# Windowed attention with sink tokens, then a rational feed-forward: attention rebuilt over head pairs with DMA transposes

## The chip, the cores and the metric

The kernel runs on one core of a Trainium2 chip. The metric is device time in microseconds (us) of one execution. The core has five engines: PE (matmul, with PEld for its weight loads), DVE (vector), ACT (scalar), POOL (GpSimd) and SP, which only issues transfers here; transfers run on the core's 16 DMA engines.

## What is computed

Four batches of eight heads, 768 positions, head dimension 64. Each position attends to the 128 positions up to itself and to the first four positions (the sinks). The attended values are laid out as 3072 tokens of 512 numbers and go through a feed-forward of width 2048, whose activation is a ratio of polynomials.

```python
scores = scale * np.matmul(q, k.transpose(0, 1, 3, 2))
keep = is_sink | in_window            # column < 4, or 0 <= row - column < 128
scores = np.where(keep, scores, -1e9)
a = softmax(scores)                   # over the last axis
x = np.matmul(a, v)                   # then heads are laid side by side: 3072 x 512
h = x @ w_in                          # 512 x 2048
P = a0 + a1*h + a2*h**2 + a3*h**3
Q = 1 + abs(b0)*abs(h) + abs(b1)*h**2
out = (P / (Q + 1e-6)) @ w_out        # 2048 x 512
```

## The kernel before

*Prologue (lines 44 to 125).* POOL builds the identity and masks, then issues the 16 transfers of `w_out` (L82), then those of the coefficients `moe_a` and `moe_b` (L86, L88). DVE computes small constants from them (L90 to L110) and casts the four pieces of `w_in` (L118), whose staging tiles `t_f` live in a pool of two buffers that is closed afterwards. The result of attention is collected in four tiles `xT`, each with the 128 columns of two heads on its partitions.

*Attention (lines 129 to 227).* One loop over batches and heads. Q, K and V of a head are loaded as 128 positions by 6 tiles (L142 and L144 on SP, L143 on ACT), cast to bf16 (L148 ACT, L149 DVE, L151 POOL), and Q and K are transposed on PE against the identity (L159, L160), six blocks each, and copied out of PSUM (L161, L162). Per head there is one matmul of the four sink keys against 512 queries (L165, exponential L168), and 11 score matmuls of 128 keys by 128 queries (L188), in three groups of two query tiles: each group has one exponential of up to 512 columns (L191) and one mask multiplication, on DVE for the first group (L195), on POOL for the two others (L198). For each query tile up to three matmuls gather the values (L203 own tile, L206 the tile before, L210 sinks), with a column of ones that gives the sum of the weights; the reciprocal (L214) scales the result (L217 on ACT or L220 on DVE), PE transposes it (L223), and once per head DVE copies it into `xT` (L226).

*Feed-forward (lines 229 to 327).* 24 units of 512 tokens by 512 hidden columns. PE multiplies by `w_in` (L258), ACT copies out (L262, tile `hb`), DVE forms numerator and denominator (L272 to L284), ACT the reciprocal by logarithm and exponential (L289, L292), DVE the product `g_t` (L321); PE multiplies by `w_out` (L300), ACT copies (L303) and SP stores (L305).

*What sets the order.* The framework places the instructions and their waits: on each engine they stand in an order that follows the program text and the readiness of operands, and an engine executes its own list in order. A tile of a pool takes over the buffer of an older tile of the same tag and waits for that tile's last reader; a pool opened after another was closed may take over its memory and waits for it.

## Time and profile before

| | us |
|---|---|
| median of 3 runs (486.37 to 487.19) | 486.61 |
| the profiled execution, whole time | 487.0 |
| its span, first to last instruction | 485.3 |
| PE busy | 392.3 |
| DVE busy | 300.5 |
| ACT busy | 295.7 |
| POOL busy | 102.3 |

Busy times are sums over instructions of one engine; a matmul's end is modelled, and matmuls overlap, so PE's time is not a measure of work at full rate. The slices divide the span in 40 equal parts, each digit a busy share in tenths. In a table by stretches, an engine's column gives busy time and the number of instructions; the last columns are the granted PE clock (1.00 is 2.4 GHz), the busy share of the DMA engines (above 1 where an engine's packets overlap) and the traffic in GB/s. In a timeline or a group an arrow names what ended the idle time ahead of the instruction.

### The profile page before, as it was taken

The numbers are of one execution on the slowest core, as the hardware profiler recorded it, in microseconds if no ns is written. First come the engines' busy times: TensorE is split into PE (matmuls) and PEld (weight loads), VectorE is DVE, ScalarE is ACT, GpSimd is POOL, SyncE is SP. The second block draws the span as 40 slices with busy tenths as digits, with TensorE's granted clock in tenths as the row PEclk, the third lists the DMA queues.
The fourth block names the chain that finished last, engine by engine and source line by source line (L and its number), as shares of the span: only waits on it lengthen the run. The fifth ranks groups of instructions, "written<-read, shape, count | busy, mean of one in ns | idle before, by whom it ended". The sixth has DMA issues, their size and how long they took to land.

```text
span 485.3 us, 6228 instructions
## 1 busy us (share of the span) xinstructions
PE 392.3 (81%) x2208; PEld 205.1 (42%) x2208; DVE 300.5 (62%) x627; ACT 295.7 (61%) x416; POOL 102.3 (21%) x155
## 2 busy tenths in 40 slices
PE   0018989887887888888897897789999999999866
PEld 0015545554554555545554533234444344443322
DVE  0223443445444445445435429999999999999970
ACT  1005645644555554555564527989979898898951
POOL 6202442424333342442434310000000000000000
PEclk9999999999999999999999999998999999999979
DMA  9778232342332242324223000001010010110102
GB/s 249 153 210 134 67 69 63 82 113 50 83 82 66 67 97 66 83 50 97 67 65 82 2 0 1 0 1 66 22 43 26 19 66 22 43 45 4 62 22 86
DMA packets 81695, 31.86 MB, mean 66 GB/s; under 512 B 76032, under 2 KB 78080, under 8 KB 81152
## 3 DMA queue, kind: packets, MB, share of 16 engines
q1 hardware_dynamic: 54208, 23.07, 17.7%
q10 hardware_dynamic: 25088, 6.29, 6.0%
q0 software_dynamic: 2368, 2.10, 2.7%
q8 instruction: 17, 0.28, 0.2%
q14 instruction: 14, 0.11, 0.1%
HBM read 27.27 MB, written 6.29 MB: 69 GB/s over the span
## 4 chain that ended last, share of the span: by engine, by line
PE 44%; DVE 40%; DMA 6%; issue 5%; ACT 3%; POOL 1%; DVEq 0%; ACTq 0%; POOLq 0%
PE ps_s L188 8%; PE ps_xall L223 7%; DVE g_t L321 5%; DVE odd L283 5%; DVE num L284 5%; PE ps_tk L160 5%; PE ps_o L203 5%; PE ps_tq L159 5%; PE ps_o L210 4%; PE ps_out L300 4%; DVE s_sq L272 4%; DVE num L281 4%; PE ps_sink L165 3%; DVE odd L278 3%; DVE den L273 3%
## 5 line engine op out<-in xcount | busy, mean ns | idle before, releaser
L300 PE MATMUL ps_out<-w_out_sb,g_t 128*128 128x512 bf16 x384 | 94.5, 395 | 16.0 <-DVE g_t L321 13.7
L258 PE MATMUL ps_h<-xT,w_in_sb 128*128 128x512 bf16 x384 | 93.8, 392 | 3.0 <-ACT hb L262 3.0
L214 DVE RECIPROCAL recip<-ps_o 128x1 f32<-128x1 f32 x192 | 29.6, 164 | 92.0 <-PE ps_o L210 84.6
L198 POOL TENSOR_TENSOR a_t<-e_t,mask_pp 128x512 bf16<-128x512 bf16 x64 | 73.9, 1161 | 59.1 <-ACT e_t L191 58.6
L160 PE MATMUL ps_tk<-ident,k_bf 128*64 128x128 bf16 x192 | 37.5, 313 | 47.3 <-DVE k_bf L149 45.6
L217 ACT ACTIVATE o_bf<-ps_o,recip 128x64 bf16<-128x64 f32 x96 | 30.0, 313 | 64.3 <-DVE recip L214 63.6
L300 PEld LDWEIGHTS <-g_t 128*128 128x128 bf16 x384 | 37.8, 101 | 68.3 <-DVE g_t L321 22.8
L191 ACT ACTIVATE e_t<-ps_s 128x512 bf16<-128x512 f32 (+1 forms) x96 | 52.4, 556 | 19.5 <-PE ps_s L188 17.0
L289 ACT ACTIVATE lnq<-den,one_eps,qsc 128x2048 f32<-128x2048 bf16 x24 | 50.3, 2096 | 19.8 <-DVE den L276 19.7
L223 PE MATMUL ps_xall<-ident,o_bf 128*64 128x128 bf16 x192 | 52.5, 314 | 9.7 <-ACT o_bf L217 5.7
L258 PEld LDWEIGHTS <-w_in_sb 128*128 128x128 bf16 x384 | 38.0, 100 | 51.2 <-issue 9.8
L262 ACT ACTIVATE hb<-ps_h 128x1024 bf16<-128x1024 f32 x48 | 48.6, 1012 | 6.0 <-PE ps_xall L223 3.3
L188 PE MATMUL ps_s<-qT,kT 64*128 64x128 bf16 x352 | 50.5, 304 | 0.2 <-ACT e_t L191 0.2
L203 PE MATMUL ps_o<-v_ext,a_t 128*128 128x65 bf16 x192 | 40.3, 237 | 8.8 <-DVE a_t L195 8.5
L160 PEld LDWEIGHTS <-k_bf 128*64 128x64 bf16 x192 | 23.5, 160 | 52.6 <-DVE k_bf L149 48.7
L292 ACT ACTIVATE rden<-lnq 128x2048 bf16<-128x2048 f32 x24 | 45.7, 1903 | 0.0
L223 PEld LDWEIGHTS <-o_bf 128*64 128x64 bf16 x192 | 24.8, 143 | 37.4 <-ACT o_bf L217 13.9
L206 PE MATMUL ps_o<-v_ext,a_t 128*128 128x65 bf16 x160 | 39.2, 245 | 0.0
L151 POOL CAST v_ext<-v_in 128x384 bf16<-128x384 f32 x32 | 16.2, 506 | 100.2 <-PE ps_o L210 67.7
L188 PEld LDWEIGHTS <-kT 64*128 64x128 bf16 x352 | 31.3, 130 | 11.8 <-issue 8.2
L159 PE MATMUL ps_tq<-ident,q_bf 128*64 128x128 bf16 x192 | 33.9, 314 | 0.0
L161 ACT ACTIVATE qT<-ps_tq 64x768 bf16<-64x768 bf16 x32 | 25.5, 797 | 13.3 <-PE ps_tq L159 10.6
(61 smaller groups left out, 495.3 us busy)
## 6 DMA issues: line engine op xcount, KB each, us to landing
q_in<-in_q_dram SPq DMA_DIRECT2D x32, 192.0 KB, 3.1
k_in<-in_k_dram ACTq DMA_DIRECT2D x32, 192.0 KB, 2.8
v_in<-in_v_dram SPq DMA_DIRECT2D x32, 192.0 KB, 2.8
out_dram<-o_t SPq DMA_DIRECT2D x24, 256.0 KB, 2.0
t_f<-in_moe_w_in_dram SPq DMA_DIRECT2D x4, 1024.0 KB, 5.7
w_out_sb<-in_moe_w_out_dram POOLq DMA_DIRECT2D x16, 128.0 KB, 5.9
a_bc<-in_moe_a_dram POOLq DMA_DIRECT2D x1, 2.0 KB, 4.5
b_bc<-in_moe_b_dram POOLq DMA_DIRECT2D x1, 1.0 KB, 4.0
```

What stands on the lines that cost most here:

```text
L159: nc.tensor.transpose(ps_tq[:, t * P:(t + 1) * P], q_bf[:, t, :], ident)
L160: nc.tensor.transpose(ps_tk[:, t * P:(t + 1) * P], k_bf[:, t, :], ident)
L188: nc.tensor.matmul(ps_s[:, co:co + P], lhsT=kT[:, kt * P:(kt + 1) * P], rhs=qT[:, t * P:(t + 1) * P], start=True, stop=True)
L191: nc.scalar.activation(out=e_t[:, 0:ncols], in_=ps_s[:, 0:ncols], func=AF.Exp)
L198: nc.gpsimd.tensor_tensor(out=a_t[:, 0:ncols], in0=e_t[:, 0:ncols], in1=pmask, op=ALU.mult)
L203: nc.tensor.matmul(ps_o, lhsT=a_t[:, col[(t, 'diag')]:col[(t, 'diag')] + P], rhs=v_ext[:, t, :], start=True, stop=(t == 0))
L223: nc.tensor.transpose(ps_xall[:, t * P:(t + 1) * P], o_bf, ident)
L258: nc.tensor.matmul(ps_h[:, j, :], lhsT=w_in_sb[c][:, fc * P:(fc + 1) * P], rhs=xT[c][:, t0:t0 + TB], start=(c == 0), stop=(c == NDMC - 1))
L262: nc.scalar.activation(out=hb[:, half * 2 * TB:(half + 1) * 2 * TB], in_=ps_h, func=AF.Copy)
L289: nc.scalar.activation(out=lnq, in_=den, func=AF.Ln, scale=qsc, bias=one_eps)
L292: nc.scalar.activation(out=rden, in_=lnq, func=AF.Exp, scale=-1.0)
L300: nc.tensor.matmul(ps_out, lhsT=g_t[:, co:co + P], rhs=w_out_sb[fc], start=(fc == 0), stop=(fc == NFFC - 1))
```

## The change

Constants, loads and the attention loop are replaced; the feed-forward keeps its text. Two heads are worked on together. K and V of a pair are held in 64-position halves: 64 partitions for one head, 64 for the other, in tiles that are zero outside the two diagonal blocks, so that one matmul over 128 rows serves both heads. A half of 64 keys is scored against the 192 queries that can see it; one exponential covers four halves (768 columns), with the scale 1/8 folded in, and one DVE multiplication masks the two 64-column edges of each half. Q, the block-diagonal K and the normalised output are transposed by DMA from SBUF to SBUF (`dma_start_transpose` on SP) instead of by PE with copies out of PSUM. The sink keys of all eight heads of a batch are gathered into one tile, and one set of matmuls gives all their scores. All loads are issued on SP. A loop of 21 steps runs the pairs in a pipeline: pair p+2 is loaded, p prepared, p-4 scored, p-5 attended and emitted. The cut diff (constants for the sinks and their V tile are left out; of removed lines the first of each block stand):

```diff
@@ -46,35 +46,37 @@
     wpool = ctx.enter_context(tc.tile_pool(name="weights", bufs=1))
     xpool = ctx.enter_context(tc.tile_pool(name="xT", bufs=1))
 
-    ident = const_pool.tile([P, P], BF16)
-    make_identity(nc, ident)
...
+
+    edge = const_pool.tile([P, 2, 64], BF16)
+    nc.gpsimd.memset(edge, 1.0)
+    for e in range(2):
+        lo = e * 64
+        nc.gpsimd.affine_select(
+            out=edge[lo:lo + 64, 0, :], in_=edge[lo:lo + 64, 0, :], pattern=[[1, 64]],
+            compare_op=ALU.is_ge, fill=0.0, base=0, channel_multiplier=-1)
+        nc.gpsimd.affine_select(
+            out=edge[lo:lo + 64, 1, :], in_=edge[lo:lo + 64, 1, :], pattern=[[-1, 64]],
+            compare_op=ALU.is_gt, fill=0.0, base=0, channel_multiplier=1)
+
...
+    with tc.tile_pool(name="a_fix", bufs=1) as a_fix, \
+         tc.tile_pool(name="a_in", bufs=3) as a_in, \
+         tc.tile_pool(name="a_q", bufs=2) as a_q, \
+         tc.tile_pool(name="a_qT", bufs=6) as a_qT, \
+         tc.tile_pool(name="a_x", bufs=3) as a_x, \
          tc.tile_pool(name="a_ps", bufs=2, space=bass.MemoryType.PSUM) as a_ps, \
-         tc.tile_pool(name="a_ps_tr", bufs=1, space=bass.MemoryType.PSUM) as a_ps_tr, \
          tc.tile_pool(name="a_ps_sink", bufs=1, space=bass.MemoryType.PSUM) as a_ps_sink, \
-         tc.tile_pool(name="a_ps_x", bufs=1, space=bass.MemoryType.PSUM) as a_ps_x, \
          tc.tile_pool(name="a_ps_o", bufs=2, space=bass.MemoryType.PSUM) as a_ps_o:
+
+        k_nat2 = []
+        for n in range(2):
+            t_ = a_fix.tile([P, NHF, P], BF16, name=f"k_bd_{n}")
+            nc.gpsimd.memset(t_, 0.0)
+            k_nat2.append(t_)
+        v_bd = []
+        for n in range(NVB):
+            t_ = a_fix.tile([P, NHF, 2, D + 1], BF16, name=f"v_bd_{n}")
+            nc.gpsimd.memset(t_, 0.0)
+            for e in range(2):
+                nc.gpsimd.memset(t_[e * 64:(e + 1) * 64, :, e, D:D + 1], 1.0)
+            v_bd.append(t_)
+        e_bd = []
+        for n in range(NEB):
+            t_ = a_fix.tile([P, 64 + NHF * EW], BF16, name=f"e_bd_{n}")
+            nc.gpsimd.memset(t_, 0.0)
+            e_bd.append(t_)
+        k_sink = []
+        for n in range(2):
+            t_ = a_fix.tile([P, NPB, P], BF16, name=f"k_sink_{n}")
+            nc.gpsimd.memset(t_, 0.0)
+            k_sink.append(t_)
...
+        def load(p):
+            b, i = p // NPB, p % NPB
+            q_in = a_in.tile([P, NT, 2, D], FP32, tag="q_in")
+            k_in = a_in.tile([P, NHF, D], FP32, tag="k_in")
+            v_in = a_in.tile([P, NHF, D], FP32, tag="v_in")
+            for e in range(2):
+                h = 2 * i + e
+                nc.sync.dma_start(out=k_in[e * 64:(e + 1) * 64],
+                                  in_=k[b, h].rearrange("(j p) d -> p j d", p=64))
+                nc.sync.dma_start(out=q_in[:, :, e, :],
+                                  in_=q[b, h].rearrange("(t p) d -> p t d", p=P))
+            for e in range(2):
+                h = 2 * i + e
+                nc.sync.dma_start(out=v_in[e * 64:(e + 1) * 64],
+                                  in_=v[b, h].rearrange("(j p) d -> p j d", p=64))
+            loaded[p] = (q_in, k_in, v_in)
+
+        def prepare(p):
+            b, i = p // NPB, p % NPB
+            q_in, k_in, v_in = loaded.pop(p)
+            q_bf = a_q.tile([P, NT, P], BF16, tag="q_bf")
+            nc.vector.tensor_copy(out=q_bf, in_=q_in.rearrange("p t e d -> p t (e d)"))
+            k_n = k_nat2[p % 2]
+            for e in range(2):
+                nc.scalar.activation(out=k_n[e * 64:(e + 1) * 64, :, e * D:(e + 1) * D],
+                                     in_=k_in[e * 64:(e + 1) * 64], func=AF.Copy)
+            qT = a_qT.tile([P, NT + 1, P], BF16, tag="qT")
+            kT = a_qT.tile([P, NHF, P], BF16, tag="kT")
+            nc.gpsimd.memset(qT[:, NT, :], 0.0)
+            nc.sync.dma_start_transpose(out=qT[:, 0:NT, :],
+                                        in_=q_bf.rearrange("p t c -> p (t c)"))
+            nc.sync.dma_start_transpose(out=kT, in_=k_n.rearrange("p j c -> p (j c)"))
+            nc.gpsimd.tensor_copy(
+                out=k_sink[b % 2][:, i, 32 * i:32 * i + 32].rearrange(
+                    "p (e s) -> p e s", e=2)[:, :, 0:NS],
+                in_=kT[:, 0, :].rearrange("p (e s) -> p e s", e=2)[:, :, 0:NS])
+            ready[p] = (qT.rearrange("p t c -> p (t c)"), kT, v_in)
+
+        def prepare_v(p):
+            v_in = ready[p][2]
+            v_n = v_bd[p % NVB]
+            for e in range(2):
+                nc.vector.tensor_copy(out=v_n[e * 64:(e + 1) * 64, :, e, 0:D],
+                                      in_=v_in[e * 64:(e + 1) * 64])
+
+        def sink_scores(b):
+            ps = a_ps_sink.tile([P, S - P], FP32, tag="ps_sink")
+            for c0, c1 in ((0, 512), (512, S - P)):
+                for i in range(NPB):
+                    nc.tensor.matmul(ps[:, c0:c1], lhsT=k_sink[b % 2][:, i, :],
+                                     rhs=ready[b * NPB + i][0][:, P + c0:P + c1],
+                                     start=(i == 0), stop=(i == NPB - 1))
+            e_s = a_x.tile([P, S - P], BF16, tag="e_sink")
+            nc.scalar.activation(out=e_s, in_=ps, func=AF.Exp, scale=inv_sqrt_d)
+            nc.vector.tensor_tensor(out=e_s[:, 0:NS], in0=e_s[:, 0:NS], in1=sink_edge,
+                                    op=ALU.mult)
+            sinks[b] = e_s
+
+        def scores(p, g):
+            qT, kT, _ = ready[p]
+            e_t = e_bd[p % NEB]
+            ps = a_ps.tile([P, 2, 512], FP32, tag="ps_s")
+            for n in range(4):
+                j = 4 * g + n
+                nc.tensor.matmul(ps[:, n // 2, (n % 2) * 192:(n % 2) * 192 + 192],
+                                 lhsT=kT[:, j, :], rhs=qT[:, 64 * j:64 * j + 192],
                                  start=True, stop=True)
-                e_sink = a_sc.tile([NS, (NT - 2) * P], BF16, tag="e_sink")
-                nc.scalar.activation(out=e_sink, in_=ps_sink, func=AF.Exp)
...
+            data = e_t[:, 64:].rearrange("p (j c) -> p j c", c=EW)
+            nc.scalar.activation(
+                out=data[:, 4 * g:4 * g + 4, 0:192].rearrange("p (a n) c -> p a n c", a=2),
+                in_=ps[:, :, 0:384].rearrange("p a (n c) -> p a n c", n=2),
+                func=AF.Exp, scale=inv_sqrt_d)
+            tri_blocks = data[:, 4 * g:4 * g + 4, :].rearrange(
+                "p j (m c) -> p j m c", c=P)[:, :, :, 0:64]
+            nc.vector.tensor_tensor(
+                out=tri_blocks, in0=tri_blocks,
+                in1=edge0 if g == 0 else edge.unsqueeze(1).to_broadcast([P, 4, 2, 64]),
+                op=ALU.mult)
+
+        def attend(p, g, x_n):
+            b, i = p // NPB, p % NPB
+            e_t = e_bd[p % NEB]
+            v_n = v_bd[p % NVB]
+            ps_o = a_ps_o.tile([P, 2, 2 * (D + 1)], FP32, tag="ps_o")
+            for n in range(2):
+                t = 2 * g + n
+                terms = []
+                for j, off in ((2 * t, 0), (2 * t - 1, 64), (2 * t + 1, -64), (2 * t - 2, 128)):
+                    if j >= 0:
+                        c = 64 + EW * j + off
+                        terms.append((e_t[:, c:c + P], v_n[:, j, :, :]))
+                if t > 0:
+                    terms.append((sinks[b][:, (t - 1) * P:t * P],
+                                  v_sink[:, b, 2 * i:2 * i + 2, :]))
+                for m, (l_, r_) in enumerate(terms):
+                    nc.tensor.matmul(ps_o[:, n, :], lhsT=l_,
+                                     rhs=r_.rearrange("p e c -> p (e c)"),
+                                     start=(m == 0), stop=(m == len(terms) - 1))
+            o4 = ps_o.rearrange("p n (e c) -> p (n e) c", e=2)
+            rec = a_x.tile([P, 4, 1], FP32, tag="rec")
+            nc.vector.reciprocal(out=rec, in_=o4[:, :, D:D + 1])
+            nc.vector.tensor_tensor(
+                out=x_n[:, 2 * g:2 * g + 2, :].rearrange("p n (e c) -> p (n e) c", e=2),
+                in0=o4[:, :, 0:D], in1=rec.to_broadcast([P, 4, D]), op=ALU.mult)
+
+        def emit_x(p, x_n):
+            b, i = p // NPB, p % NPB
+            nc.sync.dma_start_transpose(
+                out=xT[i][:, b * S:(b + 1) * S].rearrange("p (t c) -> p t c", c=P),
+                in_=x_n.rearrange("p t c -> p (t c)"))
+
+        for p in range(2):
+            load(p)
+        for p in range(NPAIR + 5):
+            if p + 2 < NPAIR:
+                load(p + 2)
+            if p < NPAIR:
+                prepare(p)
+            s_ = p - 4
+            if 0 <= s_ < NPAIR:
+                prepare_v(s_)
+                if s_ % NPB == 0:
+                    sink_scores(s_ // NPB)
+            a_ = p - 5
+            x_n = None
+            if 0 <= a_ < NPAIR:
+                x_n = a_x.tile([P, NT, P], BF16, tag="x_n", name="x_n")
+            for g in range(3):
+                if 0 <= s_ < NPAIR:
+                    scores(s_, g)
+                if x_n is not None:
+                    attend(a_, g, x_n)
+            if x_n is not None:
+                emit_x(a_, x_n)
 
     TB = 512
     NB = NTOK // TB

```

## Rows read from the trace of the kernel before

**Rows 1.** The page: busy per engine, and PE, DVE, DMA in 40 slices
```profile
PE 392.3 (81%) x2208; PEld 205.1 (42%) x2208; DVE 300.5 (62%) x627; ACT 295.7 (61%) x416; POOL 102.3 (21%) x155
...
PE   0018989887887888888897897789999999999866
...
DVE  0223443445444445445435429999999999999970
```

**Rows 2.** Busy time by stretch: us; PE, PEld, DVE, ACT, POOL; clock, DMA share, GB/s
```profile
0.00:30.30 30.30, 0.00 (x0) 0.00 (x0) 7.36 (x25) 1.49 (x2) 11.00 (x27) 1.00 0.79 208
30.30:288.00 257.70, 217.89 (x1451) 130.50 (x1452) 113.99 (x417) 133.69 (x289) 91.35 (x128) 1.00 0.34 74
288.00:470.00 182.00, 163.15 (x715) 69.99 (x713) 179.05 (x187) 158.11 (x122) 0.00 (x0) 0.97 0.08 29
470.00:485.30 15.30, 11.24 (x43) 4.58 (x43) 0.10 (x1) 2.39 (x4) 0.00 (x0) 0.83 0.18 69
```

**Rows 3.** Timelines at the stage edges: start us, us, engine, line, [idle before]
```profile
29.02 1.29 DVE L118 TENSOR_SCALAR w_in_sb<-t_f,csc 128x2048 bf16<-128x2048 f32 x1 [1.87 <-DMA t_f<-in_moe_w_in_dram]
30.33 0.38 SPq L142 DMA_DIRECT2D q_in<-in_q_dram  x1
...
287.95 1.02 ACT L262 ACTIVATE hb<-ps_h 128x1024 bf16<-128x1024 f32 x1 [3.32 <-PE ps_xall L223]
```

**Rows 4.** PE's timeline: two rounds of values, six transposes, eight wide matmuls
```profile
102.35 0.23 PE L203 MATMUL ps_o<-v_ext,a_t 128*128 128x65 bf16 x1
...
102.74 0.24 PE L203 MATMUL ps_o<-v_ext,a_t 128*128 128x65 bf16 x1
...
103.12 0.85 PE L159 MATMUL ps_tq<-ident,q_bf 128*64 128x128 bf16 x6
...
300.68 1.89 PE L258 MATMUL ps_h<-xT,w_in_sb 128*128 128x512 bf16 x8 [0.83 <-ACT hb L262]
```

**Rows 5.** Groups by shape: count, busy us, mean ns, idle us before with its releaser
```profile
L198 POOL TENSOR_TENSOR a_t<-e_t,mask_pp 128x512 bf16<-128x512 bf16 x64 | 73.9, 1161 | 59.1 <-ACT e_t L191 58.6
L191 ACT ACTIVATE e_t<-ps_s 128x512 bf16<-128x512 f32 x64 | 37.8, 594 | 16.4 <-PE ps_s L188 14.3 <-POOL v_ext L152 1.6 <-POOL v_ext L151 0.5
L220 DVE TENSOR_SCALAR o_bf<-ps_o,recip 128x64 bf16<-128x64 f32 x96 | 26.9, 280 | 2.4
L226 DVE COPY xT<-ps_xall 64x768 bf16<-64x768 bf16 x32 | 17.6, 549 | 15.8 <-PE ps_xall L223 15.0
L148 ACT ACTIVATE q_bf<-q_in 128x384 bf16<-128x384 f32 x32 | 16.4, 514 | 14.8 <-DMA q_in<-in_q_dram 14.8
L191 ACT ACTIVATE e_t<-ps_s 128x384 bf16<-128x384 f32 x32 | 15.4, 480 | 3.1 <-PE ps_s L188 2.6
```

**Rows 6.** Single lines on DVE: ns min/median/max, first and last start
```profile
L149 DVE CAST k_bf<-k_in x32: 340/360/897, 34.5 to 266.1; 128x384 bf16<-128x384 f32 x32
L195 DVE TENSOR_TENSOR a_t<-e_t,mask_p x32: 337/351/1142, 42.0 to 278.3; 128x384 bf16<-128x384 bf16 x32
```

**Rows 7.** The fastest stretch, and the densest of 256-byte loads (columns of rows 2)
```profile
4.00:6.00 2.00, 0.00 (x0) 0.00 (x0) 0.00 (x0) 0.00 (x0) 2.00 (x5) 1.00 1.01 426
35.00:42.00 7.00, 5.47 (x42) 4.23 (x42) 1.98 (x6) 2.52 (x5) 1.07 (x3) 1.00 1.35 218
```

**Rows 8.** DMA issues: count, KB each, us from issue to landing
```profile
q_in<-in_q_dram SPq DMA_DIRECT2D x32, 192.0 KB, 3.1
```

**Rows 9.** POOL's memsets: a 128-column constant, and 6 columns per head
```profile
masks.py:197 POOL MEMSET ident<- 128x128 bf16 x1 | 0.2, 204 | 0.3 <-POOLq L344 0.3
L152 POOL MEMSET v_ext<- 128x6 bf16 x32 | 4.0, 124 | 14.9 <-DVE w_in_sb L118 14.9
```

**Rows 10.** Waits of SP: line, releaser, us in total, times, longest
```profile
SPq L144 <- POOL v_ext L152: 105.7, 24, 7.5
```

**Rows 11.** PE's clock after a gap: timeline rows, then the stretch (columns of rows 2)
```profile
467.67 2.32 PE L300 MATMUL ps_out<-w_out_sb,g_t 128*128 128x512 bf16 x5 [4.04 <-DVE g_t L321]
...
470.00:474.00 4.00, 3.84 (x10) 1.45 (x11) 0.10 (x1) 0.60 (x1) 0.00 (x0) 0.52 0.12 44
```

More of the change, by code (lines that the diff above doesn't have):

```diff
@@ L63 @@
-    nc.gpsimd.affine_select(
-        out=mask_prev, in_=ones_pp, pattern=[[-1, P]], compare_op=ALU.is_gt,
-        fill=0.0, base=0, channel_multiplier=1,
-    )
-    mask_p0 = const_pool.tile([P, 3 * P], BF16)
-    nc.vector.tensor_copy(out=mask_p0[:, 0:P], in_=mask_diag)
-    nc.vector.tensor_copy(out=mask_p0[:, P:2 * P], in_=mask_diag)
-    nc.vector.tensor_copy(out=mask_p0[:, 2 * P:3 * P], in_=mask_prev)
-    nc.vector.memset(mask_p0[0:NS, 0:P], 1.0)
-    nc.vector.memset(mask_p0[0:NS, 2 * P:3 * P], 1.0)
@@ L73 @@
-    mask_pp = const_pool.tile([P, 4 * P], BF16)
-    nc.vector.tensor_copy(out=mask_pp[:, 0:P], in_=mask_diag)
-    nc.vector.tensor_copy(out=mask_pp[:, P:2 * P], in_=mask_prev)
-    nc.vector.tensor_copy(out=mask_pp[:, 2 * P:3 * P], in_=mask_diag)
-    nc.vector.tensor_copy(out=mask_pp[:, 3 * P:4 * P], in_=mask_prev)
+    edge = const_pool.tile([P, 2, 64], BF16)
[8 more added lines that the diff above has]
+            compare_op=ALU.is_gt, fill=0.0, base=0, channel_multiplier=1)
@@ new lines @@
+    edge0 = const_pool.tile([P, 4, 2, 64], BF16)
+    nc.gpsimd.tensor_copy(out=edge0, in_=edge.unsqueeze(1).to_broadcast([P, 4, 2, 64]))
+    for e in range(2):
+        nc.gpsimd.memset(edge0[e * 64:e * 64 + NS, 0, 0, :], 1.0)
+    tri = const_pool.tile([P, H, NS], FP32)
+    nc.gpsimd.memset(tri, 1.0)
+    nc.gpsimd.affine_select(out=tri, in_=tri, pattern=[[-16, H], [0, NS]],
+                            compare_op=ALU.is_ge, fill=0.0, base=0, channel_multiplier=1)
+    ind = const_pool.tile([P, H], FP32)
@@ new lines @@
+    nc.gpsimd.affine_select(out=ind, in_=tri[:, :, 0], pattern=[[16, H]],
+                            compare_op=ALU.is_ge, fill=0.0, base=NS - 1,
+                            channel_multiplier=-1)
+    nc.gpsimd.affine_select(out=tri, in_=tri, pattern=[[16, H], [1, NS]],
+                            compare_op=ALU.is_ge, fill=0.0, base=0, channel_multiplier=-1)
+    sink_edge = const_pool.tile([P, NS], BF16)
+    with nc.allow_low_precision(reason="sum of one 1 and zeros"):
+        nc.vector.tensor_reduce(out=sink_edge, in_=tri.rearrange("p h c -> p c h"),
+                                axis=mybir.AxisListType.X, op=ALU.add)
@@ L127 @@
     inv_sqrt_d = 1.0 / float(D) ** 0.5
-    with tc.tile_pool(name="a_in", bufs=2) as a_in, \
-         tc.tile_pool(name="a_tr", bufs=2) as a_tr, \
-         tc.tile_pool(name="a_sc", bufs=3) as a_sc, \
+    NHF = S // 64
+    EW = 256
+    NPB = H // 2
+    NPAIR = B * NPB
+    NQB = 6
+    NVB = 3
+    NEB = 2
+    with tc.tile_pool(name="a_fix", bufs=1) as a_fix, \
[3 more added lines that the diff above has]
+         tc.tile_pool(name="a_x", bufs=3) as a_x, \
@@ new lines @@
+        for n in range(NEB):
[7 more added lines that the diff above has]
+            k_sink.append(t_)
+        v_sink_f = a_fix.tile([P, B, H, D], FP32, name="v_sink_f")
+        nc.vector.memset(v_sink_f, 0.0)
+        for h in range(H):
+            nc.gpsimd.dma_start(out=v_sink_f[16 * h:16 * h + NS, :, h, :],
+                                in_=v[:, h, 0:NS, :].rearrange("b s d -> s b d"))
@@ new lines @@
+        v_sink = a_fix.tile([P, B, H, D + 1], BF16, name="v_sink")
+        nc.vector.tensor_copy(out=v_sink[:, :, :, 0:D], in_=v_sink_f)
+        for b in range(B):
+            nc.vector.tensor_copy(out=v_sink[:, b, :, D], in_=ind)
+        loaded, ready, scored, sinks = {}, {}, {}, {}
+        def load(p):
[14 more added lines that the diff above has]
+            loaded[p] = (q_in, k_in, v_in)
@@ new lines, in prepare_v @@
+        def prepare_v(p):
+            v_in = ready[p][2]
+            v_n = v_bd[p % NVB]
+            for e in range(2):
+                nc.vector.tensor_copy(out=v_n[e * 64:(e + 1) * 64, :, e, 0:D],
[12 more added lines that the diff above has]
+            sinks[b] = e_s
```

90 lines of the change are left out of this document (removed).

## The prediction, made before the changed kernel ran

> **What bounds the kernel now.** I read the busy shares and the 40 slices first, then one table of four stages, then single lines. The slices show two regimes: PE at 8 to 9 tenths with DVE near 4 until slice 23, after that DVE pinned at 9 [rows 1]. The stage table gives them times [rows 2]: 30.3 us of prologue with no matmul; attention to 288.0 us, where PE is busy 217.89 of 257.70 us and every other engine about half or less; the expert stage, where DVE is busy 179.05 of 182.00 us; and a tail of output matmuls. The edges rest on single rows [rows 3]: the last weight cast starts at 29.02 us and the first query load at 30.33 us, just behind it (the attention tiles take over the staging buffers' memory), and the first expert copy `hb` at 287.95 us waited for the last transpose of attention. So 485.3 = 30.3 + 257.6 + 197.4. Only attention is rewritten: 257.6 / 32 = 8.05 us per head, 16.1 us per pair of heads.
>
> **The change, part by part**, per pair of heads.
>
> *PE.* Removed: 36 transposes, 22 score matmuls, 2 sink matmuls, 30 value matmuls. Added: 12 score matmuls of 192 columns, 27 value matmuls of 130 columns, and 2 sink matmuls (8 per batch). Six 128-column transposes take 0.85 us, of which 0.31 is the last one's own time: 0.107 us each; three value matmuls of 65 columns come every 0.39 us, 0.13 each [rows 4]. A 512-column matmul takes (1.89 - 0.39) / 7 = 0.214 us [rows 4], so 64 more columns cost 0.027. New: 12 x 0.134 + 27 x 0.13 to 0.157 + about 0.4 = 5.5 to 6.2 us; I take 5.8, of the 16.1 now.
>
> *ACT.* Two copies of K (768 elements on 64 lanes): 384 elements take 0.514 us, and the exponential grows by 0.114 us for 128 more [rows 5], so 0.86 us each. Three exponentials of 768: 0.594 + 2 x 0.114 = 0.82 each. A quarter of a sink exponential, 0.18. Sum 1.7 + 2.5 + 0.2 = 4.4 us.
>
> *DVE.* A cast of 384 takes 0.340 us at least, 0.897 at worst; the masking of 384 takes 0.337 to 1.142 [rows 6]. The long ones lie beside POOL's multiply, of which 64 at 1.16 us go away [rows 5, 6]; POOL keeps small copies. I take the short ends: Q cast 0.68, two V casts 1.36, three masks of 512 elements 1.35, three reciprocals 0.5, and three normalising multiplies of 256 elements from PSUM: 0.28 us at 64 elements, 0.55 at 768 [rows 5], so at most 0.48 each, 1.4. Sum 5.3 us; with long ends about 8.
>
> So no compute engine needs more than about 6 us per pair. What is left is the transfers.
>
> *Loads.* Six of 192 KB per pair as before, still 256 bytes a piece, but all on SP. Where loads are dense the traffic stands flat at 218 GB/s with the engines' share at 1.35 [rows 7]: that is their ceiling in this shape. 1.18 MB / 218 GB/s = 5.4 us per pair.
>
> *DMA transposes.* Three per pair: Q and the output with 6 blocks of 128 x 128, K with 12, since its block-diagonal form is half zeros; 24 blocks, 786 KB. No row shows such a transfer. From below: the fastest stretch moves 426 GB/s [rows 7], 1.85 us. From above, if nothing overlaps: three transfers at the landing time of a load, 3.1 us [rows 8], about 9 us. I take the rate of the rows nearest in piece size, 218 GB/s: 3.6 us. So a pair needs 5.4 + 3.6 = 9.0 us of transfers, 7.3 to 14.4 at the ends: transfers become the bound of attention, by more than half over PE.
>
> *Prologue.* POOL's constants grow by some six small operations ahead of the `w_out` and `moe_a` transfers; at about 0.2 us each [rows 9] that is +1.3 us on the chain from those coefficients through `csc` (L97) to the weight casts, which end the prologue [rows 3]. The new zeroed tiles (15,000 elements per lane, at 204 ns per 128 [rows 9] at most 24 us, by the slope to the 6-element one about 11) are allocated first and so inherit the wait for the staging buffers, but only the first K tile gates the first transpose; the rest is hidden behind four pairs of preparation. The load buffers lie past that memory, so three pairs may load early (16 us). The DMA share is already 0.79 there [rows 2], so this delays the weights about as much; I count a third, -5.4.
>
> *Drain.* Scores of pair p are issued four iterations after its preparation, values five, and a batch's sink scores need all four of its K tiles. After the last K transpose there remain the scores of four pairs and the values of five: 4 x 1.6 + 5 x 3.9 = 26 us of PE; I take 25, and 18 if two pairs' scores get ahead. The last five output transposes (0.9 us each) fall here and not in the transfer stage, -4.5.
>
> *The sum against the profiled execution.* 31.6 + 16 x 9.0 - 4.5 - 5.4 + 25 = 190.7 us to the first `hb`, then 197.4 untouched, is a span of 388.1. That execution took 487.0 us for a span of 485.3, 1.7 around it, and the median is 0.4 lower: 389.8, stated as 389.
>
> **The rivals.**
> 1. *Slower: the transposes go in fragments.* If crossing a block breaks its 128 rows of 256 bytes into eight pieces each, at the packet rate of the loads, a block takes 32 KB / 218 GB/s x 8 = 1.2 us, a pair 28.9 + 5.4 = 34 us, and the kernel about 795 us. It decides against the change from T with 16 x (5.4 + T) = 257.6 - 25 + 8.6, T = 9.7 us per pair, 0.40 us per block. For it: nothing here prices a transpose. Against: it must be 2.7 times dearer than plain pieces.
>  The Trainium skill speaks on both sides. "VectorE: DVE Perf Modes", The three transpose paths, gives 1309 ns for a 128 x 128 block by DMA; by that the sum would be about 835 us. "Advanced Engine Details and Errata", X-Bar Transpose (TRN2), calls them as fast as regular DMAs, which is my 3.6 us or less. No row here shows either.
> 2. *SP stands in line.* All nine transfers of an iteration pass SP in order. A V load for pair p+2 takes the buffer of pair p-1, which is read only three iterations later; if it stands ahead of a transpose in SP's order, the transpose waits, and Q casts, K copies and scores wait behind it. Rows of before show the habit: SP stood 105.7 us at V loads for their buffer [rows 10], and there it cost nothing. Here some 3.5 us per pair (the landing of a transfer that overlaps nothing): D = 12.5, time about 445 us.
> 3. *PE at half clock.* After a gap of 4.04 us PE's clock was 0.52 on the mean of 470 to 474 us, about its 1.2 GHz level, and ten matmuls of 0.214 us each filled 3.84 us [rows 4, 11]. With PE idle a third of each pair this may happen throughout: 5.8 becomes about 10 us per pair, a little over the transfers, (+16 in all), and the drain doubles (+25): about 430 us. Against: the expert stage has gaps too and holds 0.97 [rows 2].
> 4. *Better overlap.* Transposes near 426 GB/s, early loads free, drain 18: 31.6 + 16 x 7.3 - 4.5 - 8 + 18 = 154; 353 us. Under that PE at about 6 us a pair is a floor.
>
> **How the numbers follow.** Forecast 50%; rival 1, 11%; rival 2, 15%; rival 3, 12%; rival 4, 11%; 1% that gains cancel. The range 350 to 450 holds all but rival 1 and tails of 2 and 4. About 0.2% can be told from no change here. Faster 0.88, same 0.01, slower 0.11.
>
> **What would show it.** Right: attention's end near 190 us, expert stage still 197 us; DMA share over 1 and SP or DMA naming most waits during attention; PE busy near 6 of 9 us; POOL nearly empty; 12.6 MB more moved. A landing time and a packet share for the transposes replace my 3.6 us. If ACT or DVE shows over 8 us per pair, my engine sums failed; if the `hb` copies start much later than the last value matmul, the hand-over did. Wrong above all: a transpose that costs far from a plain copy.

## The result, and the profile of the changed kernel

The changed kernel takes 407.76 us (median of 4 runs, 405.44 to 409.11) beside 486.49 for the kernel before on the same chip: a ratio of 0.8374, with an interval of 0.833 to 0.8418. I had forecast 389. The profiled execution took 405.44 us with a span of 403.7, where mine was 388.1: 15.6 us of the span were missed. Of the four runs of e2 below, 471.94 and 472.37 us are slow ones, and its time and ratio are those of the other two, 464.49 and 467.46.

The page: busy time, then PE, granted clock and DMA share in 40 slices of 10.1 us, then the queue that carries loads and transposes.

```profile
PE 248.1 (61%) x1403; PEld 132.8 (33%) x1424; DVE 260.8 (65%) x404; ACT 228.7 (57%) x212; POOL 40.2 (10%) x89
...
PE   0000015473318442744797697999999999999666
...
PEclk9999999595657565575899989999999999999969
DMA  8999999989999999898430001001001001001102
...
q1 hardware_dynamic: 129984, 41.96, 57.0%
```

In [rows 1] PE stood at 7 to 9 tenths through attention. Now it stands at 1 to 8, and the DMA line is full to slice 17 and then empty. The stretches, to be laid beside [rows 2] (the same columns: PE, PEld, DVE, ACT, POOL, clock, DMA share, GB/s); the edges are the first DMA transpose, two output transposes eight pairs apart, and the first `hb`:

```profile
0.00:41.40 41.40, 0.00 (x0) 0.00 (x0) 10.23 (x24) 4.85 (x6) 18.80 (x44) 1.00 1.11 226
41.40:95.00 53.60, 19.09 (x166) 14.16 (x167) 24.30 (x54) 20.55 (x26) 17.97 (x29) 0.87 1.22 181
95.00:183.00 88.00, 40.13 (x324) 32.03 (x328) 33.88 (x98) 33.67 (x42) 2.73 (x14) 0.62 1.13 180
183.00:207.10 24.10, 17.26 (x170) 12.75 (x172) 13.59 (x43) 9.36 (x13) 0.73 (x3) 0.77 0.62 120
207.10:403.70 196.60, 171.65 (x745) 73.87 (x758) 178.80 (x186) 160.27 (x126) 0.00 (x0) 0.97 0.09 34
```

In the third row eight pairs take 88 us, 11.0 us each, and no compute engine is busy for half of that: PE 5.0 us a pair, DVE 4.2, ACT 4.2. The DMA share is 1.13, where it was 0.34 in the attention of before. The expert stage is 196.6 us, as before.

SP's queue over one such pair (start, us held, line, transfer; brackets would give idle time before, and there is none):

```profile
101.11 2.10 SPq L210 DMA_TRANSPOSE qT<-q_bf  x1
103.32 2.28 SPq L212 DMA_TRANSPOSE kT<-k_bd  x1
105.65 1.28 SPq L288 DMA_TRANSPOSE xT<-x_n  x1
106.98 0.61 SPq L188 DMA_DIRECT2D k_in<-in_k_dram  x1
107.64 0.64 SPq L190 DMA_DIRECT2D q_in<-in_q_dram  x1
108.33 0.61 SPq L188 DMA_DIRECT2D k_in<-in_k_dram  x1
108.98 0.64 SPq L190 DMA_DIRECT2D q_in<-in_q_dram  x1
109.72 1.70 SPq L194 DMA_DIRECT2D v_in<-in_v_dram  x2
111.53 2.02 SPq L210 DMA_TRANSPOSE qT<-q_bf  x1
```

SP is held without a break over this pair. A load of K or Q holds it for 0.61 to 0.64 us, where one held it 0.38 in [rows 3]. Two theories fit this: SP's own issuing is the bound, or SP is held because the transfers ahead are not yet taken. The experiments decide between them.

The end of attention: the last transposes in SP's queue (six of the 16 output transposes stand behind the last K transpose), and the first copy of the expert stage, which answers to the last of [rows 3].

```profile
190.34 1.44 SPq L212 DMA_TRANSPOSE kT<-k_bd  x1
191.83 16.02 SPq L288 DMA_TRANSPOSE xT<-x_n  x6
...
207.10 1.02 ACT L349 ACTIVATE hb<-ps_h 128x1024 bf16<-128x1024 f32 x1 [4.66 <-PE ps_h L345]
```

The waits (who, for whom; us in total, times, longest; the last row is from SP's own):

```profile
PE ps L245 <- DMA kT<-k_bd: 77.5, 6, 47.8
ACT k_bd L205 <- DMA kT<-k_bd: 56.9, 9, 8.2
DVE q_bf L202 <- DMA qT<-q_bf: 31.8, 8, 6.4
...
SPq L194 <- DVE rec L281: 10.3, 4, 3.3
```

PE, ACT and DVE all wait for DMA transposes. The last row is the V load that waits for its buffer (rival 2): small, but there. The 47.8 us is PE's wait for the first K tiles, before any matmul.

### The profile page after: what moved, and what is told of

It reads as the page before. It is cut to its first block, busy times and chain, and to the rows that moved or that the text cites. A ratio compares the mean times of both kernels' runs of the same rounds, so it can differ in the third digit from the quotient of the medians.

```text
span 403.7 us, 4046 instructions
## 1 busy us (share of the span) xinstructions
PE 248.1 (61%) x1403; PEld 132.8 (33%) x1424; DVE 260.8 (65%) x404; ACT 228.7 (57%) x212; POOL 40.2 (10%) x89
## 2 busy tenths in 40 slices
DMA packets 132629, 44.36 MB, mean 110 GB/s; under 512 B 126944, under 2 KB 129024, under 8 KB 132096
## 4 chain that ended last, share of the span: by engine, by line
DVE 44%; DMA 16%; PE 15%; SPq 10%; issue 6%; POOL 5%; ACT 4%; POOLq 0%; DVEq 0%; ACTq 0%
DMA kT<-k_bd 7%; DVE g_t L408 6%; DVE odd L370 6%; DVE num L371 6%; PE ps_o L276 6%; PE ps_out L387 5%; DVE s_sq L359 5%; DVE num L368 4%; DVE odd L365 4%; DMA q_in<-in_q_dram 4%; SPq L210 3%; DVE den L360 3%; DVE den L363 2%; SPq L188 2%; DVE x_n L282 2%
## 5 line engine op out<-in xcount | busy, mean ns | idle before, releaser
L245 PE MATMUL ps<-qT,kT 128*128 128x192 bf16 x192 | 32.5, 306 | 86.1 <-DMA kT<-k_bd 77.5
L205 ACT ACTIVATE k_bd<-k_in 64x768 bf16<-64x768 f32 x32 | 26.9, 841 | 71.3 <-DMA kT<-k_bd 56.9
L249 ACT ACTIVATE e_bd<-ps 128x768 bf16<-128x768 f32 x48 | 37.2, 809 | 39.2 <-PE ps L245 23.1
L276 PE MATMUL ps_o<-v_bd,e_bd 128*128 128x130 bf16 x352 | 39.5, 265 | 10.4 <-DVE x_n L282 6.3
L276 PEld LDWEIGHTS <-e_bd 128*128 128x128 bf16 x352 | 30.8, 120 | 16.7 <-DVE x_n L282 8.9
L255 DVE TENSOR_TENSOR e_bd<-e_bd,edge 128x512 bf16<-128x512 bf16 x48 | 19.2, 413 | 21.3 <-ACT e_bd L249 21.3
L408 DVE TENSOR_TENSOR g_t<-num,rden 128x2048 bf16<-128x2048 bf16 x24 | 29.4, 1226 | 0.1
L371 DVE TENSOR_TENSOR num<-num,odd 128x2048 bf16<-128x2048 bf16 x24 | 29.4, 1226 | 0.0
L370 DVE TENSOR_TENSOR odd<-odd,hb 128x2048 bf16<-128x2048 bf16 x24 | 29.4, 1226 | 0.0
L363 DVE TENSOR_TENSOR den<-den,s_sq 128x2048 bf16<-128x2048 bf16 x24 | 29.4, 1226 | 0.0
L359 DVE TENSOR_TENSOR s_sq<-hb 128x2048 bf16<-128x2048 bf16 x18 | 22.1, 1226 | 3.3 <-ACT hb L349 3.3
L223 DVE CAST v_bd<-v_in 64x768 bf16<-64x768 f32 x32 | 20.0, 624 | 5.8 <-PE ps_o L276 3.9
```

Source lines behind the costliest of these rows:

```text
L245: nc.tensor.matmul(ps[:, n // 2, (n % 2) * 192:(n % 2) * 192 + 192], lhsT=kT[:, j, :], rhs=qT[:, 64 * j:64 * j + 192], start=True, stop=True)
L276: nc.tensor.matmul(ps_o[:, n, :], lhsT=l_, rhs=r_.rearrange("p e c -> p (e c)"), start=(m == 0), stop=(m == len(terms) - 1))
L359: nc.vector.tensor_tensor(out=s_sq, in0=hb, in1=hb, op=ALU.mult)
L363: nc.vector.tensor_tensor(out=den, in0=den, in1=s_sq, op=ALU.add)
L370: nc.vector.tensor_tensor(out=odd, in0=odd, in1=hb, op=ALU.mult)
L371: nc.vector.tensor_tensor(out=num, in0=num, in1=odd, op=ALU.add)
```

## The experiments

The theory (A): the traffic of the DMA engines, loads and transposes together, sets the step of 11 us. The rivals: SP's issuing, one instruction after the other (B); the V loads that wait for their buffer (C); PE at half clock (D); a prologue that starts late (E). e1 to e4 ran on one chip, e5 to e12 on another; the kernel before took 486.5 us on the first and 486.6 to 487.9 on the second.

**e1: all loads issued by ACT.** If SP's list is the bound, this frees it.

```diff
-                nc.sync.dma_start(out=k_in[e * 64:(e + 1) * 64],
+                nc.scalar.dma_start(out=k_in[e * 64:(e + 1) * 64],
...
-                nc.sync.dma_start(out=v_in[e * 64:(e + 1) * 64],
+                nc.scalar.dma_start(out=v_in[e * 64:(e + 1) * 64],
```

The load of `q_in` between them is changed likewise.

> Only the issuer of the six loads of a pair changes, from SP to ACT; traffic is the same. Theory A (the DMA engines are full: 5.4 us of loads and about 5 us of transposes per pair make the 10.7 us steps): nothing is gained, 405 to 411 us. Theory B (SP's own issue time is the step: four loads at 0.61 to 0.64 us, two V loads at 1.7 together, three transposes at 1.3 + 2.0 + 2.4 are 10 us of the 10.7): SP keeps under 6 us per pair, the step falls to about 9 us, 27 us in all, to about 380 us; ACT rises from 4.4 to about 8 us per pair.

Measured: 430.76 us, ratio 0.8856 (0.8823 to 0.8889), 23 us slower than the changed kernel. ACT's timeline shows why:

```profile
123.42 0.66 ACTq L188 DMA_DIRECT2D k_in<-in_k_dram  x1
131.55 1.31 ACTq L194 DMA_DIRECT2D v_in<-in_v_dram  x2
132.90 0.74 ACTq L190 DMA_DIRECT2D q_in<-in_q_dram  x1
133.68 1.69 ACT L205 ACTIVATE k_bd<-k_in 64x768 bf16<-64x768 f32 x2 [9.87 <-issue]
```

The V load was held from 124 to 131.55 us, and the K copy that stood behind it in ACT's list waited 9.87 us with nothing else to blame. The wait moved from a queue with nothing else to do to an engine that feeds the transposes. The run does not tell A from B, since it brought in a new wait, but it shows what a waiting load costs in the wrong list.

**e2: all loads issued by POOL**, in the same three places.

```diff
-                nc.sync.dma_start(out=k_in[e * 64:(e + 1) * 64],
+                nc.gpsimd.dma_start(out=k_in[e * 64:(e + 1) * 64],
...
```

> The same six loads issued by POOL, which is empty in attention. Theory A: 405 to 411 us, as with ACT. Theory B: about 380 us, and if ACT's issue time hurts its exponentials, less than with ACT. Either way slower than with ACT if POOL needs more than 1.5 us to issue one such load (16 issues of w_out took it 0.55 us each, with half as many pieces or fewer).

Measured: 466.0 us, ratio 0.9575 (0.9527 to 0.9623). In the trace, which is that of a run of 471.94 us, POOL needs 0.79 to 0.89 us on the mean to issue one of these loads, and it stood 39.5 us at V loads that waited for their buffer, up to 13.2 at a time; the copy `k_sink` (L213) and the next loads stood behind. POOL is nearly empty as an engine and still a bad place for the loads.

**e3: Q transposed twice**, the second time into a tile that nobody reads: 96 more blocks of 128 x 128 in 16 more transfers.

```diff
+            qT_more = a_more.tile([P, NT, P], BF16, tag="qT_more")
+            nc.sync.dma_start_transpose(out=qT_more,
+                                        in_=q_bf.rearrange("p t c -> p (t c)"))
```

> Every Q is transposed a second time into a tile that nobody reads: 96 more blocks of 128 x 128. It prices a transposed block. My 3.6 us per 24 blocks: 0.9 us per pair, +14 us. The steps of the changed kernel (10.7 less 5.4 of loads is 5.3 per 24 blocks): 1.3 us per pair, +21 us, 429 us. If SP's hold is what counts (2.0 us for a Q transpose at the median): +32 us, 440 us. A price near 1.3 us per block would be +125 us.

Measured: 429.04 us, ratio 0.8811 (0.8774 to 0.8847): +21.3 us, 1.33 us for each transfer of six blocks, with no compute added. So a transpose added lies on the path. This alone does not tell A from B: SP holds a Q transpose for 1.2 us even where no load stands near it (1.23 at 189.01 us of the changed kernel), and 16 of these would be 19 us.

**e4: eight V buffers instead of three**, so that no V load waits.

```diff
+         tc.tile_pool(name="a_v", bufs=8) as a_v, \
...
-            v_in = a_in.tile([P, NHF, D], FP32, tag="v_in")
+            v_in = a_v.tile([P, NHF, D], FP32, tag="v_in")
```

> V's loads get eight buffers instead of three, so none waits for a pair that is read three iterations later. SP stood at V loads three times for some 4 us (at 79, 122 and 166 us). If each of these stops the transfers in full: -12 us, 396 us. If the transfers that were already queued cover them (the steps with a stop took 11.5 us against 10.7 without): -3 us or no change, 404 to 408 us.

Measured: 402.87 us, ratio 0.8271 (0.824 to 0.8303): -4.9 us, and the waits of V loads are gone from SP. C is real and worth about 5 us. The runs that follow stand on top of e4, or on the run that they name.

**e5: K transposed in six blocks**, without the zeros; POOL then copies the two halves into tiles that were zeroed once. K is loaded as Q is, and ACT copies it in one instruction instead of two.

```diff
-            nc.sync.dma_start_transpose(out=kT, in_=k_n.rearrange("p j c -> p (j c)"))
+            nc.sync.dma_start_transpose(out=k6, in_=k_bf.rearrange("p t c -> p (t c)"))
+            for e in range(2):
+                lo = e * 64
+                nc.gpsimd.tensor_copy(
+                    out=kT[lo:lo + 64, :, lo:lo + 64],
+                    in_=k6[lo:lo + 64].rearrange("p t (u c) -> p (t u) c", u=2))
```

> On top of the eight V buffers (402.9 us): K is loaded and transposed as Q is, six blocks per pair instead of twelve, and POOL copies the two diagonal halves into tiles that were zeroed once. At the price that the doubled Q transpose gave (21 us for 96 blocks): -21 us, 382 us. At my 3.6 us per 24 blocks: -14 us, 388 us. If only SP's hold counted (K 2.4 us against Q 1.9 to 2.0): -8 us, 395 us. POOL's copies add a latency of some 2 us per pair, which four pairs of lead cover.

Measured: 389.2 us, ratio 0.7991 (0.7961 to 0.802): -13.7 us, 0.86 us for six blocks fewer in the same number of transfers. This is the clearest evidence for A: the number of SP's issues is the same and the bytes went. A shorter issue of the K transpose does not explain it: with no loads left, one of twelve blocks holds SP for 1.44 us (e4, the last) and one of six for 1.21 (e5, the last), which over 16 pairs is 3.7 us.

**e6: K and V loads by ACT, Q loads left on SP**: e1's diff without the `q_in` line.

> On top of the eight V buffers (402.9 us): the four loads of K and V are issued by ACT, Q's two and the transposes by SP. With the buffers no load stands waiting for a reader three iterations away. Theory A (the engines' traffic sets the 10.7 us step): 400 to 405 us. Theory B (SP's issue time): about 383 us, down to the engines' 9.4 us. In between if only the half microsecond counts in which the engines fall to a share of 0.10 behind each output transpose: -10 us, 392 us.

Measured: 416.05 us, ratio 0.8553, 13 us slower than e4. ACT's K copies now wait for transposes (25.5 us for `kT`, 20.6 for `xT`) with loads behind them in ACT's list, and SP waits 36.0 us at the output transpose for DVE. The share of the DMA engines fell from 1.06 to 0.82 (100 to 200 us of the changed kernel and of e6). Two thirds of e1's move, something over half of its cost.

**e7: the staging buffers of `w_in` kept to the end**, so that the attention tiles inherit no wait for them.

```diff
-    with tc.tile_pool(name="w_stage", bufs=2) as w_stage:
+    w_stage = ctx.enter_context(tc.tile_pool(name="w_stage", bufs=2))
```

> On top of the eight V buffers (402.9 us): the pool of the w_in staging tiles stays open, so the zeroed tiles of attention have memory of their own and POOL zeroes them from about 18 us instead of 36 us. First K transposes at 25 to 30 us instead of 45.6. If the traffic alone counts, only what the engines were idle before 45 us comes back: -4 us, 399 us. If the late start of the transposes is a delay of its own (I had put the start at 31.6 us): -10 to -14 us, 389 to 393 us.

Measured: 404.9 us, ratio 0.8321 (0.8275 to 0.8368), no difference from e4 that can be told. The first Q transpose still came at 43.36 us, behind the last weights and the loads of three pairs in SP's list, not behind the buffers. E falls as far as the buffers go.

**e8: the output transposed on PE and evacuated by DVE, as before the change.**

```diff
-            nc.sync.dma_start_transpose(
-                out=xT[i][:, b * S:(b + 1) * S].rearrange("p (t c) -> p t c", c=P),
-                in_=x_n.rearrange("p t c -> p (t c)"))
+            ps_x = a_ps_x.tile([P, NT, P], BF16, tag="ps_x")
+            for t in range(NT):
+                nc.tensor.transpose(ps_x[:, t, :], x_n[:, t, :], ident)
+            nc.vector.tensor_copy(out=xT[i][:, b * S:(b + 1) * S],
+                                  in_=ps_x.rearrange("p t c -> p (t c)"))
```

> On top of the eight V buffers (402.9 us), one part undone: the output is transposed by PE against an identity and copied to xT by DVE; sink scores share the score buffers in PSUM. Six blocks fewer by DMA in the eleven steps that hold an output transpose: 11 x 1.3 = -14 us, and one DMA less at the end, 388 us. PE gains 0.65 us (1.3 at its half clock), DVE 0.55 us per pair, both beside the transfers. If PE at the half clock is what sets the step, it gets slower: 408 to 412 us.

Measured: 395.09 us, ratio 0.8108 (0.8079 to 0.8138): -7.8 us, 0.49 us per transfer taken away, about a third of what one added cost in e3. The direction supports A, and this part of the change costs time: with it undone the kernel is faster. The traces tell why the gain was small. The last K transposes of e3, e4 and e8:

```profile
209.28 1.44 SPq L216 DMA_TRANSPOSE kT<-k_bd  x1
188.07 1.44 SPq L213 DMA_TRANSPOSE kT<-k_bd  x1
178.43 1.46 SPq L215 DMA_TRANSPOSE kT<-k_bd  x1
```

Only ten output transposes stand ahead of the last K transpose, and from e4 to e8 it comes 9.6 us earlier, 0.96 us for each. The first `hb` (205.73 and 198.22 us) came 17.7 us behind it in e4 and 19.8 in e8, which gives 2.1 back. In e3 the last K transpose came 18.9 us later than in the changed kernel, 1.18 us for each transfer added; the rest of the 21.3 lies behind it.

**e9: on e5, the two Q loads of a pair as one DMA of 384 KB, the K loads too:** the same bytes in four issues instead of six. B expects the two saved issues back, A expects nothing.

```diff
-            for e in range(2):
-                h = 2 * i + e
-                nc.sync.dma_start(out=k_in[:, :, e, :],
-                                  in_=k[b, h].rearrange("(t p) d -> p t d", p=P))
...
+            nc.sync.dma_start(out=k_in, in_=k[b, 2 * i:2 * i + 2].rearrange(
+                "e (t p) d -> p (e t) d", p=P))
```

> On top of K in six blocks and eight V buffers (389.2 us): the two heads' loads of Q become one DMA of 384 KB, those of K too; bytes, pieces and queue are the same, SP issues four loads per pair instead of six. Theory A (traffic sets the step): 386 to 392 us, no change. Theory B (SP's issue time, 0.62 us a load): two issues less in sixteen pairs, -20 us, 369 us; if the issue time goes by pieces and not by instructions, this run cannot tell and shows no change with issues of twice the length.

Measured: 387.05 us, ratio 0.7951 (0.7923 to 0.7979), the interval overlapping e5's. SP's queue of e5, then of e9, over one pair:

```profile
132.71 0.58 SPq L189 DMA_DIRECT2D k_in<-in_k_dram  x1
133.34 0.53 SPq L191 DMA_DIRECT2D q_in<-in_q_dram  x1
133.91 0.54 SPq L189 DMA_DIRECT2D k_in<-in_k_dram  x1
134.50 0.77 SPq L191 DMA_DIRECT2D q_in<-in_q_dram  x1
135.32 1.68 SPq L195 DMA_DIRECT2D v_in<-in_v_dram  x2
```

```profile
127.07 0.58 SPq L187 DMA_DIRECT2D k_in<-in_k_dram  x1
127.70 0.68 SPq L189 DMA_DIRECT2D q_in<-in_q_dram  x1
128.43 2.87 SPq L193 DMA_DIRECT2D v_in<-in_v_dram  x2
```

The six loads of e5 hold SP for 4.3 us (132.71 to 137.00); the four of e9 hold it for 4.2 (127.07 to 131.30): what two issues saved comes back as a longer hold of the V loads. So the hold is not a price per issue, and B falls. That it is back-pressure of full engines is the likely reading. Whether the one queue in which all nine transfers now stand has a part in it was not tested: before, loads came by SP's queue and ACT's, and e1 and e6, which bring the second queue back, brought new waits as well.

**e10: PE kept at work**, with four 512-column matmuls behind each group of value matmuls into a tile that nobody reads.

```diff
                 if x_n is not None:
                     attend(a_, g, x_n)
+                    fill(4)
```

> On top of the eight V buffers (402.9 us): behind each group of value matmuls PE runs four 512-column matmuls of constants into a spare bank, 2.6 us per pair at full clock, which keep it from idling (the sink scores share the score buffers to free the bank). The granted clock of attention should rise from 0.65 towards 1.0. If the half clock is hidden behind the transfers: 400 to 406 us. If PE's slow matmuls were part of the step: -10 us or more, 393 us or less. If the added work is in the way: slower, 410 us or more.

Measured: 409.23 us, ratio 0.8377 (0.8325 to 0.8429), 6 us slower than e4. The first row is e4, the second e10, over the same stretch (columns as above):

```profile
95.00:180.00 85.00, 38.26 (x325) 30.05 (x328) 33.84 (x98) 33.89 (x42) 2.66 (x14) 0.65 1.16 184
```

```profile
95.00:180.00 85.00, 44.60 (x410) 34.76 (x411) 42.15 (x125) 39.43 (x50) 3.51 (x17) 0.74 1.16 173
```

The clock rose from 0.65 to 0.74 and the DMA share stayed at 1.16. The first `hb` went from 205.73 to 213.18 us. So a higher clock, bought with twelve dead matmuls a pair, did not shorten the transfers. The dead matmuls take PE's time too (45.9 us in all), so the run does not price the clock by itself; that PE was busy for under half of each pair at the low clock speaks against D more than e10 does.

**e11: e9 with the output on PE**, by the diff of e8.

> K in six blocks, output transposed by PE, eight V buffers and merged loads of Q and K together. Transfers per pair: 5.4 us of loads, Q and K transposes at 0.9 to 1.3 each, 7.2 to 8.0 us against 10.7. Sum of the single gains (-13.7 and -7.8 from 402.9): 381 us without a gain by merging; about 361 us with it. PE at the lower clock (6.5 us of work becomes up to 13) may become the step instead: then not under 385 us.

Measured: 387.16 us, ratio 0.7958 (0.7923 to 0.7992), no better than e9. The step did fall, from 9.2 to 8.0 us, and the last K transpose was issued at 167.62 us. But the first `hb` came at 187.51, as in e9 (187.92): 20 us behind the last K transpose, where the changed kernel needs 17. POOL, which zeroes six K tiles in this version, started late:

```profile
PE ps L239 <- POOL k_sink L221: 81.2, 7, 67.7
...
POOL kT_bd L153 <- DVE w_in_sb L122: 17.8, 1, 17.8
```

**e12: e11 with the staging buffers kept**, by the diff of e7, which takes away the cause of that last row: POOL zeroes from 18.31 us on, instead of from 36.98. What had bought nothing in e7 is tried where POOL's zeroing stands in the path.

> On top of e11 (K in six blocks, Q and K merged loads, output transposed on PE): the staging buffers of w_in stay allocated to the end, so POOL's zeroed tiles lie in other memory and need not wait for the last weight cast. In e11 POOL began zeroing at 36.98 us, did its first K copies at 64.07, and the DMA share was 0.29 from 60 to 70 us because the first scores, and with them SP's later transposes, stood behind POOL. If that late start is the loss: first K copy about 12 to 16 us earlier, no stretch of low share before 150 us, first hb near 178 and about 377 us. If the bound has gone over to the drain on PE and DVE (20 us in e11) or to DVE all along, the early start only lengthens a later wait: 384 to 388 us.

Measured: 382.02 us (381.57 to 383.29), ratio 0.7845 (0.7818 to 0.7872), the fastest version, and 26 us faster than the changed kernel. POOL's first K copy came at 51.88 us instead of 64.07, but the first `hb` only 4.0 us earlier (183.53), between the two expectations. In e12 the DMA share is 1.03 from 120 to 160 us against 1.28 from 100 to 120: the transfers no longer fill the engines throughout. Which of PE, DVE and the order of the lists takes the other 8 us is open.

## Why the prediction came out as it did

**Right: what bounds it.** The bound went from PE to the transfers, which pace attention (e5, e9, and e3 with them), and the first guess of the engines' work holds. Predicted against measured, from the groups (count, busy us, mean ns): the copies of K at 0.86 us each, the exponentials at 0.82, the masks at 0.45, the Q cast at 0.68.

```profile
L205 ACT ACTIVATE k_bd<-k_in 64x768 bf16<-64x768 f32 x32 | 26.9, 841 | 71.3 <-DMA kT<-k_bd 56.9
L249 ACT ACTIVATE e_bd<-ps 128x768 bf16<-128x768 f32 x48 | 37.2, 809 | 39.2 <-PE ps L245 23.1
L202 DVE CAST q_bf<-q_in 128x768 bf16<-128x768 f32 x16 | 11.7, 728 | 49.1 <-DMA qT<-q_bf 31.8
L255 DVE TENSOR_TENSOR e_bd<-e_bd,edge 128x512 bf16<-128x512 bf16 x48 | 19.2, 413 | 21.3 <-ACT e_bd L249 21.3
```

Taking the short ends of [rows 6] was right; that they are short because POOL's multiply went is likely, and no run put it back. The traffic is 44.36 MB, 12.5 more than before, as forecast, and the expert stage is 196.6 us, forecast at 197.4.

**Right: the start of the transfers.** My sum had 31.6 us of prologue and 10.8 us left of the early loads, 42.4 us in all, before the first transpose. It was issued at 41.44. The sum was luckier than its terms: the last weight cast ended at 36.1 us instead of 31.6, and what stood between it and the first transpose was 5.3 us instead of 10.8.

**Wrong in size: the transfers.** From there to the last K transpose in place I had 13 x 5.4 for loads and 16 x 3.6 - 4.5 for transposes, 123.3 us. The last K transpose was issued at 190.34; with 3.7 us, the shortest landing of one, it is there at 194.0, so 152.6 us, 29.3 more. The step that failed is "I take the rate of the rows nearest in piece size", for loads and transposes one after the other: a rate has no price per transfer, and none for time in which nothing moves. e5 gives six blocks in size alone, 0.86 us, 0.143 a block, where I had 0.15: the rate of the blocks was right. e3 gives six blocks with a transfer of their own, 1.33. The difference, 0.47 us (0.2 to 0.7 by the intervals of the four medians), is an estimate of what a transfer costs beside its size, and a high one: e3 stands on three V buffers, and its waits for them are longer than the changed kernel's. By the last K transposes, e8's 0.96 less e5's 0.86 leaves 0.1.

Of the 48 transposes 42 fall into the stretch, ten of them outputs, where my sum had eleven. They make 4 us at the low price and 20 at the high one, and the V loads' wait (e4) is 5 more; what is left of the 29.3, some 5 to 20 us, no run prices.

The trace shows where time goes in which little moves. One step of the changed kernel, cut by hand where the traffic changes (columns as above, the last two are DMA share and GB/s):

```profile
108.40:115.40 7.00, 1.84 (x11) 1.19 (x9) 0.42 (x1) 1.61 (x2) 0.00 (x0) 0.50 1.40 188
115.40:116.00 0.60, 0.00 (x0) 0.00 (x0) 0.00 (x0) 0.00 (x0) 0.00 (x0) 0.50 0.23 42
116.00:117.40 1.40, 0.00 (x0) 0.00 (x0) 0.52 (x1) 0.00 (x0) 0.00 (x0) 0.50 1.28 283
117.40:117.80 0.40, 0.00 (x0) 0.00 (x0) 0.04 (x1) 0.00 (x0) 0.00 (x0) 0.50 0.55 115
117.80:118.90 1.10, 0.42 (x2) 0.15 (x3) 0.00 (x0) 0.65 (x1) 0.19 (x1) 0.50 0.89 171
118.90:119.40 0.50, 0.50 (x5) 0.34 (x3) 0.00 (x0) 0.48 (x2) 0.14 (x2) 0.50 0.10 18
```

By the bytes, the first row is the six loads and the Q transpose together (7.0 us x 188 GB/s = 1.32 MB, for 1.38), the third the K transpose (1.4 x 283 = 396 KB, for 393), the fifth the output transpose (188 KB, for 197). Between them lie three gaps of 0.4 to 0.6 us with hardly any traffic, 1.5 us in all, while SP has the next transfer in hand (the K transpose from 113.65, the output transpose from 116.70, loads from 118.04). This step of 11.0 is thus 1.5 of gaps that I had not, 0.4 less than I had for K (1.8), 0.2 more for the output (0.9), and 0.7 more for loads and Q (6.3).

Not every step has all three. Over the eight pairs from 95 to 183 us, read in stretches of 0.2 us, the share was under 0.5 for 12.0 us in all, and 5.5 of these stand around two waits of SP for a V buffer:

```profile
125.60:128.20 2.60, 2.18 (x32) 1.78 (x30) 2.16 (x8) 2.14 (x3) 0.54 (x2) 0.98 0.02 5
168.90:171.80 2.90, 2.74 (x33) 2.40 (x32) 2.28 (x9) 2.00 (x3) 0.19 (x1) 0.80 0.02 4
```

DVE, whose cast (L223) reads the V tile and frees its buffer, was busy for 2.16 and 2.28 us, PE for 2.18 and 2.74: there the transfers waited for the compute engines. The other 6.5 us are 0.8 a pair, where the step shown has 1.5. The 88 us moved 15.8 MB, which is 72.7 us at 218 GB/s: of the 15 us between, 12.0 are gaps and 3 a lower rate. That a transfer behind a transpose waits for its end is a reading of the gaps that no run shows: with one transpose in three gone they hardly fell (from 95 to 170 us 7.6 us in e4, 1.1 a pair, and 7.4 in e8, 1.0). The cause of the gaps beside the V waits stays open.

**Wrong in size, the other way: the drain.** I took 25 us behind the last K transpose; it is 13.1 (194.0 to 207.10). From 192 us on PE still had 28 score matmuls (2.3 pairs at 12) and 98 value matmuls (3.6 pairs at 27), not four pairs and five: with each pair late by its transfers, PE had caught up with most of what could be done, and its clock was 1.00 from 194 us on. The low end that I had named, 18, was the nearer. So the sum of the errors is +29.3 - 11.9 - 1.0 at the start = +16.4 at the first `hb` (207.1 against 190.7). The total looks better than its terms are.

**The rivals.** Fragments (1) are out: at 0.143 us a block nothing comes near the 0.40 from which the change would have lost. (The 795 and 835 us there leave the last five outputs at 0.9 us each; at the rival's own price they would be some 30 and 35 us lower.) The Trainium skill's figure of 1309 ns for a block ("VectorE: DVE Perf Modes", The three transpose paths) is not what a block costs in a transfer of six or twelve here: e3 and e5 give 0.14 to 0.22 us, and the measurement decides. Its other sentence ("Advanced Engine Details and Errata", X-Bar Transpose (TRN2)), that they are as fast as regular DMAs, agrees in the rate of e5's blocks, 32 KB / 0.143 us = 229 GB/s beside 218 for loads [rows 7]; e3's 1.33 us for six blocks in a transfer of their own is 148 GB/s. SP's line (2) happened at 5 us instead of the 56 that I had priced: it stops the transfers only every fourth pair (V loads at 83.61, 126.78 and 170.37 us). Half clock (3) happened in full, 0.62 from 95 to 183 us, and was priced wrongly. PE was busy 5.0 us a pair even so, under my 10 and under the step, so but for the V waits it lay in the shadow of the transfers. Better overlap (4) did not come.

## What to carry to other kernels

When transposes move from PE to DMA, price the transfers by their bytes at the rate of the loads beside them, add something for each transfer and for the stretches in which none can run (the rate alone gave 123 us where 153 were measured), and do not transpose zeros: leaving out the zero half of K was worth 13.7 us. Then ask which transposes the engine that has become idle can take back: the outputs on PE were worth 7.8 us (e8); Q and K on PE were not tried. When a queue seems to be the bound, merge its issues before its loads are moved elsewhere: if the hold grows by what was saved (e9), the issues are not the bound. And a load that waits for a buffer does least harm in a list that has nothing else to do (e1, e2, e6). A sum of two serial stages, transfers and drain, can come near in total with both terms wrong, so each edge is to be read from the trace.
